# Window attention and a mixture of experts on one core: logits evicted ahead of values, values in block order, rows requested later

## The chip, the cores and the metric

The kernel runs on one core of one Trainium2 chip. A core has five engines that run their own instruction streams side by side: TensorE (PE; its weight loads are listed apart as PEld), VectorE (DVE), ScalarE (ACT), GpSimd (POOL) and SyncE (SP), which here issues most of the DMAs. Matmul results land in PSUM, everything else is in SBUF. The metric is the device time of one execution in microseconds (us).

## The reference

```python
# q, k, v: 8 batches x 8 heads x 576 positions x 64; N = 8*576 = 4608 tokens, D = 512, E = 8 experts, F = 1024
scores = (1 / np.sqrt(64)) * q @ k.transpose(0, 1, 3, 2)
rel = pos[:, None] - pos[None, :]
scores = np.where((rel >= 0) & (rel < 64), scores, -1e9)     # each position sees itself and the 63 before it
attn = softmax(scores)                                       # with 1e-9 added to the sum
x = (attn @ v).transpose(0, 2, 1, 3).reshape(N, D)

logits = x @ w_gate + modality_bias[modality_id]
e_idx = np.argmax(logits, axis=1)
gate_w = softmax(logits)[np.arange(N), e_idx]
for e in range(E):                                           # each token goes to one expert
    mask = e_idx == e
    out[mask] = gate_w[mask, None] * (np.maximum(x[mask] @ w1[e], 0) @ w2[e])
```

## The kernel before

**Attention.** The tokens are cut into 72 blocks of 64 positions; two neighbouring blocks make a pair of 128 tokens, and there are `NPR` = 36 pairs. The main loop (`for s in range(NPR + 4)`) is a software pipeline written out by hand: step s computes scores and their row minima for pair s (`scores`, `minima`), the exponentials (`exps`), the transposed probabilities of pair s-1 (`probs_t`, into `pT`), the products with the values of pair s-2 (`values`, eviction in `values_out`) and their transposes (`x_t`), and the gate's logits of pair s-3 (`logits`). Queries and keys of later pairs are transposed in between (`heads_t`, `heads_out`, into `qT` and `kT`). The program order on every engine is the order in which these functions are called; no scheduler reorders it.

`values` writes `av`, one PSUM bank of 128 tokens x 8 heads x 64. Its 32 matmuls (16 heads' halves for the upper, 16 for the lower 64 partitions; these two halves run side by side) write 64 neighbouring columns each, so that `av` is ordered by head. `values_out` takes the reciprocal of the 8 row sums `rs` and multiplies `av` by it into `xa`, in two VectorE instructions, one for each half a of a head's 64 columns. On the way it changes the order of the columns: `xa` holds, for g = head modulo 2 and a = first or second 32 columns of the head, 128 columns from the four heads of that g:

```python
to = xa[:, 0:DM].rearrange("p (g a c d) -> p a c g d", g=2, a=2, d=R32)
```

`x_t` then transposes the four blocks of 128 columns of `xa`, ScalarE copies them out as `xaT`, and a step later `logits` multiplies them by the gate's weights and adds the bias on VectorE into `lg` (line L694), out of PSUM. That PSUM tile is one of two that take turns under the name `tp` (`turn_bank`); in a step from 13 on the turns are: logits, probabilities for the first half of the heads, probabilities for the second half, the transposes of xa, then heads and routing. The second half's transposes so reuse the bank of the logits and have to wait for the eviction of those.

In a step, VectorE was given `values_out`, then the eviction of the logits, then the eight minima.

**Routing.** Every second step the logits of two pairs choose the experts (`route1` to `route3`), and the 256 rows `xa`, with gate and token number in two more columns, are scattered by an indirect DMA of GpSimd into `xs_scratch`, sorted by expert (L765).

**Experts.** A slot is 256 rows of one expert, computed in 16 pieces. Piece `first(k, i)` is 12 matmuls of the first layer (L304, into `em` or `sp`), piece `second(k, t)` 6 matmuls of the second (L326, into `y`). Weights and rows are split into a high and a low part (`Whi`, `Wlo`, `xh`, `xl`), and three products of parts are added up. The generator `slot_pieces` yields after each piece; from step `FIRST` = 12 on, each attention step has four gaps, and each `gap` runs one piece, so that a slot takes four steps. What follows a piece on the other engines goes through the list `later`. When the attention is over, the remaining slots run without gaps (there `last` is set).

The weights of two experts are loaded and split in the attention steps by `weights(s)`, in units of 128 x 512 (DMAs of L103 and L107 on SP, splits L114 on ScalarE and L119 on VectorE).

The rows of the next slot are requested by `fetch()` while the present slot is computed: SP reads the row number that VectorE worked out (L204) and issues five DMAs from `xs_scratch` into the tile `xt` (L211), of which there is one. Later `x_turn` transposes `xt` in 32 x 32 blocks on VectorE (L266), and `x_part` splits it into `xh` and `xl` (L195, L196) and has GpSimd copy gate and token number (L287, L289). Which slots may run during attention is fixed by `EARLY`: the table for a slot is worked out after the step that scattered its rows. The requests fall in steps 11, 14, 18, 22, 26, 30, 34 and 38; the slots of steps 14, 18 and 22 are planned in the step just before. A request on SP has to wait until the scatter of its rows has landed. In a slot of the attention steps, `fetch` stands before piece `first(2, 1)`, which is the second gap of its step, and `x_turn` follows piece `first(3, 1)`, in the second gap of the next step. Once `last` is set, `fetch` stands before `first(1, 0)`.

Of the kernel before, what the change touches and what calls it, by code (L numbers as in the profile page):

```python
# [8 lines left out]
F32 = mybir.dt.float32  # L9
# [4 lines left out]
ALU = mybir.AluOpType  # L14
# [5 lines left out]
P = 128  # L20
W64 = 64
# [5 lines left out]
def tile_window_attn_moe(  # L27
# [12 lines left out]
    nc = tc.nc  # L40
    B, H, S, D = q.shape
    N = B * S
    DM = H * D
    E = w_gate.shape[1]
    F = w1.shape[2]
    HP = H // 2
    R32 = 32
# [3 lines left out]
    NPR = NBLK // 2  # L51
# [15 lines left out]
    FIRST = 12  # L67
# [7 lines left out]
    NC1 = DM // P  # L75
# [153 lines left out]
    todo = []  # L229
    last = []  # L230
# [37 lines left out]
    def slot_pieces():  # L268
# [129 lines left out]
        NK = NC2 // 2  # L398
# [10 lines left out]
        while True:  # L409
            nxt = None  # L410
            for k in range(1, NK):
                for i in range(2):
                    if (k, i) == ((1, 0) if last else (2, 1)) or k == 2 and i == 1 and nxt is None:
                        assert todo
                        nxt = fetch()
                    first(sl, k, i)
                    if k == NK - 1 and i == (0 if last else 1):
                        later.append(lambda: x_turn(nxt))
                    yield
                for t in range(2):  # L420
                    second(sl, k - 1, t)
                    if k == NK - 1 and nxt and t == 1:
                        x_part(nxt, 1)
                    yield
                    if k == NK - 1 and nxt and t == 0:
                        x_part(nxt, 0)
                        run_later()
            second(sl, NK - 1, 0)
            yield
            if nxt["nb"] == 1:  # L430
                break
            first(nxt, 0, 0)
            yield
            first(nxt, 0, 1)
            yield
            second(sl, NK - 1, 1)
            yield
            sl = nxt
# [40 lines left out]
    small = actx.enter_context(tc.tile_pool(name="small", bufs=2))  # L479
# [18 lines left out]
    vo = {}  # L498
    ve = {}
    qk = {}  # L500
    st = {}
# [148 lines left out]
        nc.gpsimd.tensor_scalar(out=rs, in0=sm, scalar1=1e-9, scalar2=None, op0=ALU.add)  # L650


    def values(p):
        st.pop((p, "s"))
        av = st[p, "av"] = ps_a.tile([P, H, D], F32, name="av")
        for u in range(H):
            a, hp = divmod(u, HP)
            pT = st[p, "p", a]
            for c in range(2):
                i = hp * P + c * W64  # L660
                nc.tensor.matmul(  # L661
                    out=av[c * W64:(c + 1) * W64, 2 * hp + a], lhsT=pT[:, i:i + W64],
                    rhs=(vo if c else ve)[p][:, 2 * hp + a, :], start=True, stop=True)

    def values_out(p):
        rs = st.pop((p, "rs"))
        nc.vector.reciprocal(out=rs, in_=rs)
        xa = st[p, "xa"] = xas[p % XBUF]
        av = st.pop((p, "av")).rearrange("p (c g) (a d) -> p a c g d", g=2, a=2)
        to = xa[:, 0:DM].rearrange("p (g a c d) -> p a c g d", g=2, a=2, d=R32)  # L670
        for a in range(2):
            nc.vector.tensor_tensor(  # L672
                out=to[:, a], in0=av[:, a],
                in1=rs.rearrange("p (c g) -> p c g", g=2)[:, :, :, None].broadcast_to([P, NC1, 2, R32]), op=ALU.mult)

    def x_t(p, xp):
        xa = st[p, "xa"]
# [337 lines left out]
    for s in range(NPR + 4):  # L1015
        j = s % GB
        for f, args in at.pop(s, ()):
            f(*args)
        n_tick = 6 if s < FIRST else 5
        n_gap = 0 if s < FIRST else 4  # L1020
        G = s // GB + 1
        heads = PARTS[j] if G < NG else ()
        R = (s - 5) // GB if s >= 5 and j == 1 else -1
        if 1 <= s < FIRST:
            swap_upper(s - 1)

        if 2 <= s < NPR + 2:
            values(s - 2)
            values_out(s - 2)
        if 3 <= s < NPR + 3:  # L1030
            logits(s - 3, turn_bank(s) if s != FIRST else ps_m.tile([P, 512], F32, name="y0"))
            if (s - 3) % GB == GB - 1:
                route1((s - 3) // GB)
        if s < NPR:
            scores(s)
            if s == FIRST:
                x_turn(fetched[0])
                gap(it, True)
            minima(s)
            if s == FIRST - 2:  # L1040
                tick(todo[0][-1] - issued[0], table=True)
        if 1 <= s <= NPR:
            if s == FIRST:
                run_later()
            if s >= FIRST:
                swap_upper(s - 1)
            swap_v(s - 1)
            for a in range(2):
                probs_t(s - 1, a, turn_bank(s))
            sums(s - 1)  # L1050
        if s < NPR:
            exps(s, (0, 1))
        if s == 0:
            first_pair(1, (both[:1], both[1:]))
            cast_bias()
        if n_gap > 0 and s != FIRST:
            gap(it, True)
        if 2 <= s < NPR + 2:
            x_t(s - 2, turn_bank(s) if s != FIRST else ps_m.tile([P, 512], F32, name="y0"))
        run_later()  # L1060
        tick(2)
        if s < NPR:
            exps(s, (2, 3, 4))
        if n_gap > 0:
            if FIRST < s < FIRST + 4 or s % 2:
                weights(s)
            if s != FIRST:
                gap(it, True)
        if heads:
            tp = turn_bank(s)  # L1070
            heads_t(G, *heads[0], tp)
            heads_out(tp, G, *heads[0], nc.vector.tensor_copy)
        if s == FIRST:
            weights(s)
            gap(it, True)
        run_later()
        tick(n_tick)
        cnt = None
        if R >= 0:
            tp = turn_bank(s)  # L1080
            rk = route2(R, tp)
            if R == NG - 1 or any(R == T for T, _ in EARLY):
                cnt = counts_out(tab if R == NG - 1 else pl, counts(R, tp))
            route3(R, rk)
        if s < NPR:
            exps(s, (5, 6, 7))
        if n_gap > 2:
            if FIRST <= s < FIRST + 4:
                weights(s)
            gap(it, True)  # L1090
        if heads:
            tp = turn_bank(s)
            heads_t(G, *heads[1], tp)
            heads_out(tp, G, *heads[1], nc.scalar.copy if heads[1] == K1 else nc.vector.tensor_copy)
        run_later()
        tick(n_tick)
        if s == WEIGHTS:
            load_weights()
        if s >= WEIGHTS:
            weights(s)  # L1100
        if n_gap > 3:
            gap(it, True)
        run_later()
        if s == 1:
            select_bias()
        if s == 4:
            nc.sync.dma_start(out=xs_blk[DUMMY:DUMMY + 2].rearrange("b p c -> p b c"), in_=padrow)
        for T, xs_ in EARLY:
            if T == R:
                plan(T, xs_, cnt)  # L1110
# [270 lines left out]
```

## Time and profile before

| | |
|---|---|
| time, median of 3 runs | 629.67 us (629.13 to 629.82) |
| time of the profiled execution | 629.68 us |
| span of the profiled execution, first to last instruction | 627.8 us |
| mean granted TensorE clock | 0.994 |
| TensorE busy | 605.6 us (96%) |
| VectorE busy | 383.7 us (61%) |
| ScalarE busy | 298.5 us (48%) |
| GpSimd busy | 138.2 us (22%) |
| HBM traffic | 67.49 MB read, 23.91 MB written, 146 GB/s over the span |

Busy times of engines overlap, and a busy time is a sum over the whole program. The page also cuts the span into 40 equal slices and gives each engine's busy share of a slice in tenths. Attention alone takes about the first 81 us (steps 0 to 12), attention with experts' pieces goes on to about 352 us (steps 12 to 39), and the experts alone to the end. In a list of waits a line reads: engine, tile and line that waited, what released it, total us, how often, the longest. In a timeline a line reads: start, time taken, engine, line, operation, tiles (out<-in), shape, count, and in brackets the idle time before it and its releaser. Matmul ends are modelled.

### The profile page before, as it was taken

Reading aid. Unit: us, or ns where it says so; the run is one execution under the profiler, and the core shown is the slowest. Engines: PE = TensorE matmul, PEld = TensorE weight load, DVE = VectorE, ACT = ScalarE, POOL = GpSimd, SP = SyncE. Lnnn points to the kernel's source line nnn. Section 1 sums busy time; section 2 is a strip of 40 time slices with the busy share of each in tenths; the row PEclk is TensorE's granted clock in tenths of the full one; section 3 lists DMA queues with packets and bytes.
Section 4 is the critical chain, followed back from the end, with each engine's and each line's share of the span. In section 5 each row is a group of like instructions: output and inputs, shape, how many; then the busy total and the mean of one; then the engine's idle time right before and its main releaser. Section 6 shows DMA issues by size and latency. Waiting matters only on the chain.

```text
span 627.8 us, 17328 instructions
## 1 busy us (share of the span) xinstructions
PE 605.6 (96%) x6365; PEld 541.8 (86%) x6365; DVE 383.7 (61%) x1522; ACT 298.5 (48%) x933; POOL 138.2 (22%) x315
## 2 busy tenths in 40 slices
PE   8998879999999999999999999999999999999996
PEld 5887778889889888888988999999999999989986
DVE  4889988867766776757665275223324633876721
ACT  4899876665657556555644111111113522564411
POOL 6332322042222212320422220011011111102202
PEclk7999999999999999999999999999999999999999
DMA  9999864864674654553422133622062544677300
GB/s 164 207 229 238 203 186 139 212 170 120 169 202 124 177 125 112 143 135 87 128 61 84 53 102 101 226 78 69 13 190 78 164 162 124 194 247 234 125 13 24
DMA packets 158982, 88.07 MB, mean 140 GB/s; under 512 B 122618, under 2 KB 141616, under 8 KB 158768
## 3 DMA queue, kind: packets, MB, share of 16 engines
q1 hardware_dynamic: 150272, 67.45, 42.9%
q0 software_dynamic: 5888, 18.93, 8.0%
q8 instruction: 50, 0.82, 0.5%
q10 hardware_dynamic: 2736, 0.58, 0.5%
q14 instruction: 36, 0.29, 0.2%
HBM read 67.49 MB, written 23.91 MB: 146 GB/s over the span
## 4 chain that ended last, share of the span: by engine, by line
PE 50%; DVE 0%; issue 0%; POOL 0%; ACT 0%; POOLq 0%
PE y L326 23%; PE em L304 13%; PE sp L304 10%; PE tp L467 1%; PE y L377 1%; PE av L661 1%; PE sp L352 0%; PE em L352 0%; PE tp L689 0%; PE sp L609 0%; DVE xa L672 0%; POOL out_dram L390 0%; ACT pT L644 0%; POOLq L1258 0%; DVE y L388 0%
## 5 line engine op out<-in xcount | busy, mean ns | idle before, releaser
L326 PE MATMUL y<-Whi,hh 128*128 128x512 f32 x288 | 117.0, 406 | 0.0
L635 ACT ACTIVATE ss<-ss,mn 128x128 f32<-128x128 f32 x288 | 112.4, 396 | 5.2 <-DMA y<-in_moe_modality_id_dram 2.8
L326 PE MATMUL y<-Wlo,hh 128*128 128x512 f32 x288 | 112.8, 392 | 0.0
L326 PE MATMUL y<-Whi,hl 128*128 128x512 f32 x288 | 112.7, 391 | 0.0
L337 POOL DMA_INDIRECT out_dram<-y,id x36 | 39.8, 1104 | 238.0 <-DVE y L334 156.6
L313 DVE SCALAR_TENSOR_TENSOR hl<-em,hh 128x512 fp32r<-128x512 f32 x50 | 34.5, 690 | 92.9 <-ACT hh L312 91.4
L304 PE MATMUL em<-xh,Whi 128*128 128x256 f32 x400 | 83.8, 291 | 0.0
L312 ACT ACTIVATE hh<-em 128x512 fp32r<-128x512 f32 x50 | 29.5, 591 | 105.3 <-PE em L304 101.3
L304 PE MATMUL em<-xl,Whi 128*128 128x256 f32 x400 | 79.3, 280 | 0.0
L304 PE MATMUL em<-xh,Wlo 128*128 128x256 f32 x400 | 79.2, 280 | 0.0
L623 DVE CUSTOM_DVE_ANT_0 ss<-sp,masks 128x128 f32<-128x128 f32 x288 | 63.5, 286 | 7.2 <-PE sp L609 7.1
L644 ACT COPY pT<-tp 128x512 f32<-128x512 f32 x57 | 32.0, 588 | 75.3 <-PE tp L467 75.2
L326 PEld LDWEIGHTS y<-Whi,hl 128*128 128x128 f32 x288 | 54.1, 188 | 12.1
L304 PEld LDWEIGHTS em<-xh,Whi 128*128 128x128 f32 x400 | 62.4, 189 | 1.8
L326 PEld LDWEIGHTS y<-Whi,hh 128*128 128x128 f32 x288 | 54.2, 188 | 8.2
L326 PEld LDWEIGHTS y<-Wlo,hh 128*128 128x128 f32 x288 | 54.3, 188 | 7.8
L304 PEld LDWEIGHTS em<-xl,Whi 128*128 128x128 f32 x400 | 61.0, 188 | 0.0
L304 PEld LDWEIGHTS em<-xh,Wlo 128*128 128x128 f32 x400 | 60.9, 188 | 0.0
L635 ACT ACTIVATION_READ_ACCUMULATOR ss<-ss,mn 128x1 f32 x288 | 55.4, 192 | 0.0
L765 POOL DMA_INDIRECT xs_scratch<-xa,idx x36 | 36.3, 1009 | 84.9 <-DVE lm L708 27.2
L312 ACT ACTIVATE hh<-sp 128x512 fp32r<-128x512 f32 x22 | 13.2, 598 | 75.8 <-PE sp L304 75.8
L661 PEld LDWEIGHTS av<-ve,pT 128*64 128x64 f32 x576 | 36.3, 138 | 13.1 <-issue 7.5
(240 smaller groups left out, 1215.5 us busy)
## 6 DMA issues: line engine op xcount, KB each, us to landing
xt<-xs_scratch SPq DMA_DIRECT2D x72, 128.0 KB, 2.8
vo<-in_v_dram SPq DMA_DIRECT2D x32, 256.0 KB, 3.3
y<-in_moe_w_dram SPq DMA_DIRECT2D x32, 256.0 KB, 3.4
vo<-in_moe_w_dram SPq DMA_DIRECT2D x24, 256.0 KB, 4.6
ss<-in_moe_w_dram SPq DMA_DIRECT2D x24, 256.0 KB, 3.3
xs_scratch<-xs_scratch SPq DMA_DIRECT2D x8, 514.0 KB, 5.5
pT<-in_moe_w_dram SPq DMA_DIRECT2D x16, 256.0 KB, 4.2
qk<-in_k_dram SPq DMA_DIRECT2D x14, 256.0 KB, 4.0
```

The source lines that it names most:

```text
L304: nc.tensor.matmul(out=hb[:, i * TP:(i + 1) * TP], lhsT=w[buf][:, c0:c0 + P], rhs=x[:, c * TP:(c + 1) * TP], start=(n == 0), stop=(n == le ...
L312: nc.scalar.activation(out=hh, in_=hb, func=AF.Relu),
L313: nc.vector.scalar_tensor_tensor(out=hl, in0=hb, scalar=0.0, in1=hh.bitcast(F32), op0=ALU.max, op1=ALU.subtract)))
L326: nc.tensor.matmul(out=sl["y", t], lhsT=h[:, i * TP + t * P:i * TP + (t + 1) * P], rhs=w[buf][:, c0:c0 + DM], start=(k == 0 and n == 0), s ...
L337: ins = nc.gpsimd.indirect_dma_start(out=out, out_offset=bass.IndirectOffsetOnAxis(ap=sl["id"][:, t:t + 1], axis=0), in_=y, in_offset=None ...
L377: nc.tensor.matmul(out=yp[:, cols], lhsT=sl["h", n][lo][:, c * P:(c + 1) * P], rhs=w[buf][:, c0 + cols.start:c0 + cols.stop], start=(m == ...
L467: nc.tensor.transpose(out=out_, in_=in_, identity=ident[p0:p0 + n, p0:p0 + n])
L623: nc.vector.tensor_tensor_reduce(out=ss[a][:, hp, :], in0=sp[a][:, hp * P:(hp + 1) * P], in1=mask, scale=-1.0 / 8.0, scalar=3.0e38, op0=AL ...
L635: nc.scalar.activation(out=ss[a][:, hp, :], in_=ss[a][:, hp, :], func=AF.Exp, bias=mn[:, h:h + 1], scale=-1.0, accum_out=sm[:, h:h + 1])
L644: nc.scalar.copy(out=pT, in_=pp)
L661: nc.tensor.matmul(out=av[c * W64:(c + 1) * W64, 2 * hp + a], lhsT=pT[:, i:i + W64], rhs=(vo if c else ve)[p][:, 2 * hp + a, :], start=Tru ...
L765: ins = nc.gpsimd.indirect_dma_start(out=xs, out_offset=bass.IndirectOffsetOnAxis(ap=idx[:, j:j + 1], axis=0), in_=xg[j], in_offset=None)
```

## The change

Three edits, in one diff:

- `values` writes the products into `av` in the column order of `xa`, as two runs of 32 columns for each matmul. `values_out` then needs one multiplication of 128 x 512 in place of two of 128 x 256. The reciprocals are written four-fold ordered (16 instead of 8 for each token) so that they can be broadcast over runs of 32 columns.
- From step 13 on, `values_out` is called after `logits` (and `route1`, which only puts work on a list), not before. Up to step 12 the order stays.
- In the attention steps, `fetch` moves from before `first(2, 1)` to before `second(1, 1)`, from the second gap of its step to the fourth. `x_turn` stays where it was.

```diff
@@ slot_pieces
             for k in range(1, NK):
                 for i in range(2):
-                    if (k, i) == ((1, 0) if last else (2, 1)) or k == 2 and i == 1 and nxt is None:
-                        assert todo
+                    if k == 1 and i == 0 and last:
                         nxt = fetch()
+                        turn_at = 0
                     first(sl, k, i)
-                    if k == NK - 1 and i == (0 if last else 1):
+                    if k == NK - 1 and i == turn_at:
                         later.append(lambda: x_turn(nxt))
                     yield
                 for t in range(2):
+                    if k == 2 and t == 1 and nxt is None:
+                        nxt = fetch()
+                        turn_at = 1
                     second(sl, k - 1, t)
...
+    def by_block(x):
+
+        return x.rearrange("p h d -> p (h d)").rearrange("p (g a c d) -> p g a c d", g=2, a=2, d=R32)
+
     def values(p):
...
                 nc.tensor.matmul(
-                    out=av[c * W64:(c + 1) * W64, 2 * hp + a], lhsT=pT[:, i:i + W64],
-                    rhs=(vo if c else ve)[p][:, 2 * hp + a, :], start=True, stop=True)
+                    out=by_block(av)[c * W64:(c + 1) * W64, a, :, hp, :], lhsT=pT[:, i:i + W64],
+                    rhs=(vo if c else ve)[p][:, 2 * hp + a, :].rearrange("p (a d) -> p a d", a=2),
+                    start=True, stop=True)

     def values_out(p):
         rs = st.pop((p, "rs"))
-        nc.vector.reciprocal(out=rs, in_=rs)
+        rw = small.tile([P, 2, 2, HP], F32, name="rw")
+        nc.vector.reciprocal(
+            out=rw, in_=rs.rearrange("p (c g) -> p g c", g=2)[:, :, None, :].broadcast_to([P, 2, 2, HP]))
         xa = st[p, "xa"] = xas[p % XBUF]
-        av = st.pop((p, "av")).rearrange("p (c g) (a d) -> p a c g d", g=2, a=2)
-        to = xa[:, 0:DM].rearrange("p (g a c d) -> p a c g d", g=2, a=2, d=R32)
-        for a in range(2):
-            nc.vector.tensor_tensor(
-                out=to[:, a], in0=av[:, a],
-                in1=rs.rearrange("p (c g) -> p c g", g=2)[:, :, :, None].broadcast_to([P, NC1, 2, R32]), op=ALU.mult)
+        nc.vector.tensor_tensor(
+            out=xa[:, 0:DM].rearrange("p (x d) -> p x d", d=R32),
+            in0=st.pop((p, "av")).rearrange("p h d -> p (h d)").rearrange("p (x d) -> p x d", d=R32),
+            in1=rw.rearrange("p g a c -> p (g a c)")[:, :, None].broadcast_to([P, 2 * H, R32]), op=ALU.mult)
@@ main loop
         if 2 <= s < NPR + 2:
             values(s - 2)
-            values_out(s - 2)
+            if s <= FIRST:
+                values_out(s - 2)
         if 3 <= s < NPR + 3:
             logits(s - 3, turn_bank(s) if s != FIRST else ps_m.tile([P, 512], F32, name="y0"))
             if (s - 3) % GB == GB - 1:
                 route1((s - 3) // GB)
+        if FIRST < s < NPR + 2:
+            values_out(s - 2)
         if s < NPR:
             scores(s)
```

## Prediction

> **What bounds the kernel now.** I read the page first (busy time and the slices), then the windows by stage, then the waits of the stage in which TensorE idles, and last the timeline around those waits.
>
> ```profile
> PE 605.6 (96%) x6365; PEld 541.8 (86%) x6365; DVE 383.7 (61%) x1522; ACT 298.5 (48%) x933; POOL 138.2 (22%) x315
> PE   8998879999999999999999999999999999999996
> ```
> ```profile
> 20.00:81.00 61.00, 53.28 (x1025) 46.81 (x1024) 55.85 (x313) 54.55 (x212) 22.93 (x44) 1.00 0.95 224
> 81.00:352.00 271.00, 264.17 (x3392) 236.12 (x3392) 188.61 (x880) 158.08 (x548) 64.84 (x134) 1.00 0.51 136
> 352.00:609.00 257.00, 257.00 (x1671) 234.15 (x1668) 124.43 (x260) 73.59 (x134) 35.41 (x76) 1.00 0.43 131
> ```
>
> The window columns are stretch, length, and busy time of PE, PEld, DVE, ACT, POOL, then granted clock, DMA share and GB/s. There are three stages. From 352 us on (experts alone) PE is busy without a break at the full clock: this change has nothing to win there, and whatever earlier stages save arrives there unchanged. From 81 to 352 us (attention steps 13 to 37 with the experts' pieces between them) PE idles 271.00 - 264.17 = 6.8 us. Before 81 us (attention alone, steps 2 to 12) DVE is busy 55.85 of 61 us, more than PE.
>
> What PE and DVE wait for in the middle stage, and DVE's waits in the first (us in total, times, longest):
>
> ```profile
> DVE xa L672 <- PE av L661: 8.9, 11, 1.2
> DVE ss L623 <- PE sp L609: 5.4, 12, 0.5
> PE tp L467 <- DVE lg L694: 5.2, 8, 1.6
> PE tp L467 <- ACT pT L644: 3.4, 3, 2.0
> ```
> ```profile
> DVE xa L672 <- PE y L467: 1.5, 1, 1.5
> DVE ss L623 <- PE sp L609: 0.6, 1, 0.6
> DVE xa L672 <- PE av L661: 0.4, 1, 0.4
> ```
>
> So 5.2 of the 6.8 us in which PE stands still are eight transposes of probabilities that wait for the logits' eviction (L694), because they use the same PSUM bank. In the first stage DVE waits only 1.5 + 0.6 + 0.4 = 2.5 us, so nearly every DVE nanosecond saved there moves the whole program.
>
> **The change, part by part.**
>
> *1. Logits evicted first (steps 13 to 37).* The worst case is step 13: DVE comes late out of an expert's eviction, then does reciprocal, two halves of xa, and only then L694. The DVE rows, and the PE row that waits:
>
> ```profile
> 87.98 0.69 DVE L313 SCALAR_TENSOR_TENSOR hl<-em,hh 128x512 fp32r<-128x512 f32 x1 [0.82 <-ACT hh L312]
> 88.59 0.19 DVE L667 RECIPROCAL rs<-rs 128x8 f32<-128x8 f32 x1
> 88.87 0.88 DVE L672 TENSOR_TENSOR xa<-av,rs 128x256 f32<-128x256 f32 x2
> 89.67 0.15 DVE L694 TENSOR_TENSOR lg<-tp,bias_sel 128x8 f32<-128x8 f32 x1
> 89.74 0.28 DVE L623 CUSTOM_DVE_ANT_0 ss<-sp,masks 128x128 f32<-128x128 f32 x1
> ```
> ```profile
> 89.88 0.55 PE L467 MATMUL tp<-ident_r,ss 128*128 128x128 f32 x3 [1.55 <-DVE lg L694]
> 166.50 0.63 PE L467 MATMUL tp<-ident_r,ss 128*128 128x128 f32 x4 [1.09 <-DVE lg L694]
> 307.15 0.66 PE L467 MATMUL tp<-ident_r,ss 128*128 128x128 f32 x4 [0.20 <-DVE lg L694]
> ```
>
> L694 would take the reciprocal's place at 88.59 instead of 89.67: 1.08 us earlier. Of the eight waits only the first, 1.55, is longer than what is gained by that (0.47 stays); the second longest, 1.09, goes but for a hundredth; the last is the shortest. Upper bound: 5.2 - 0.5 = 4.7 us. Lower bound: 0, if PE merely meets another wait as early. What is late next: in these steps DVE is behind, and its own chain behind L694 (minima, then ScalarE's exponentials) hardly moves, so PE comes up to 1 us nearer to it. The waits list has no PE wait on kT, qT, hh or hl, and DVE is busy only 188.61 of 271 us, so I take most of it: 4.0 us.
>
> The price of the new order falls in the steps in which DVE is early and waits for values. Step 18:
>
> ```profile
> 141.57 0.19 DVE L667 RECIPROCAL rs<-rs 128x8 f32<-128x8 f32 x1
> 142.34 0.88 DVE L672 TENSOR_TENSOR xa<-av,rs 128x256 f32<-128x256 f32 x2 [0.57 <-PE av L661]
> 143.14 0.15 DVE L694 TENSOR_TENSOR lg<-tp,bias_sel 128x8 f32<-128x8 f32 x1
> 143.77 0.29 DVE L623 CUSTOM_DVE_ANT_0 ss<-sp,masks 128x128 f32<-128x128 f32 x1 [0.48 <-PE sp L609]
> ```
> ```profile
> 142.09 0.59 PE L689 MATMUL tp<-wg,xaT 128*64 128x8 f32 x16
> 142.61 1.10 PE L609 MATMUL sp<-kT,qT 64*64 64x128 f32 x32
> ```
>
> Now DVE idles until the logits end (142.09 + 0.59 = 142.68) with reciprocal, xa and minima queued behind. It runs L694 (89.74 - 89.67 = 0.07 until the next starts), the reciprocal (0.28 until xa may start, plus 0.05, below) and one eviction (0.60, below): 142.75 + 0.07 + 0.33 + 0.60 = 143.75, with some 0.07 taken for the signal from PE. The minima begin at 143.77 in any case, as they wait for the scores. Cost: nothing, with only hundredths of a microsecond of cover; without cover it would be some 0.5 us of DVE per such step, on an engine with 82 us free in this stage. I cost it at 0. The x transposes come a quarter step later. POOL and SP get no instruction from the moved function, so neither queue is reordered by this part.
>
> *2. One eviction for two, and a wider reciprocal (all 36 steps).*
>
> ```profile
> L672 DVE TENSOR_TENSOR xa<-av,rs x72: 424/425/426, 20.1 to 345.8; 128x256 f32<-128x256 f32 x72
> L667 DVE RECIPROCAL rs<-rs x36: 179/196/204, 19.8 to 344.9; 128x8 f32<-128x8 f32 x36
> ```
> ```profile
> L759 DVE RECIPROCAL xa<-se x36: 143/150/166, 39.2 to 363.8; 128x1 f32<-128x1 f32 x36
> ```
>
> Two evictions hold DVE from 88.87 to 89.67 = 0.80 us. A 512-wide one from PSUM holds it for 88.59 - 87.98 = 0.61 (the L313 row; I use 0.60). The reciprocal goes from 8 to 16 elements: (196 - 150)/7 = 6.6 ns an element, so +0.05. Net: 0.80 - 0.60 - 0.05 = 0.15 us a step. In steps 2 to 12 this is 11 x 0.15 = 1.6 us, of which I take 1.4, since DVE does wait at a few points there. From step 13 on it falls into DVE's free time: 0. The x transposes now wait for the whole eviction instead of its first half, but the whole ends 0.15 us before the second half did, and two of the four blocks needed that half anyway: 0.
>
> [...]
>
> *3. Strided products (L661).* Each product writes two runs of 32 columns instead of one of 64. No row shows TensorE writing runs. The nearest shows it reading them: half of the scores (L609, window of c = 0) read two blocks in descending order, half one piece, and all take the same:
>
> ```profile
> L609 PE MATMUL sp<-kT,qT x1152: 268/269/473, 8.4 to 326.7; 64*64 64x128 f32 x192
> ```
> ```profile
> 334.17 1.08 PE av L661 x32
> 343.60 1.08 PE av L661 x32
> ```
>
> Lower bound 0; a gain has no reason, as the columns stay. Upper bound: a run costs as much as a whole product of 64 columns, which doubles 1.08 us a step: over the 25 steps from 13 to 37, in which PE is the bound, 27 us. I take 0 by the scores' row, and keep part of the rest for the range.
>
> *4. Rows requested two pieces later.* This moves one register load and five DMAs on SP behind one or two weight loads, and the table's DVE instructions with them. The first slot of this kind:
>
> ```profile
> 108.23 2.48 SPq L211 DMA_DIRECT2D xt<-xs_scratch  x5
> 110.97 0.36 SPq L107 DMA_DIRECT2D y<-in_moe_w_dram  x1
> 111.63 1.02 SPq L103 DMA_DIRECT2D y<-in_moe_w_dram  x1
> ```
> ```profile
> SPq L211 <- DMA xs_scratch<-xa,idx: 11.2, 4, 4.2
> ```
> ```profile
> POOL gate L287 <- DMA xt<-xs_scratch: 35.7, 7, 7.2
> ```
> ```profile
> xt<-xs_scratch SPq DMA_DIRECT2D x72, 128.0 KB, 2.8
> ```
> ```profile
> 117.00 1.29 DVE L266 STREAM_TRANSPOSE xt<-xt 128x512 f32<-128x512 f32 x2
> ```
>
> The requests already sit up to 4.2 us on the scatter of the rows they read; two pieces (half of a step of 343.60 - 334.17 = 9.4 us, so some 5) mostly replace that wait, and let weight loads pass. Issued by 108.23 + 2.48 = 110.7 and landing 2.8 us later, the rows are there near 114 and needed at 117.00: 3 us of cover. The delay beyond today's is 5 - 4.2, so some 1 to 2 us: hidden, 0. GpSimd waits for the rows too (gate), and would wait that much longer; behind it on POOL is the next step's ve copy, which the products need only a step later. A gain has no place to appear, as neither PE nor DVE waits for a weight load in the lists above.
>
> **Sum.** 629.68 us is the profiled execution's time, 1.9 us more than its span of 627.8, and within 0.01 of the median 629.67. 629.7 - 4.0 - 1.4 = 624.3 us.
>
> **Rivals.**
>
> *A. The wait is only handed on.* PE, freed from L694, meets the next thing late: pT from ScalarE (already 3.4 us) or x transposes behind a later xa. For it: DVE gains 0.15 us a step where PE gains up to 1.08. Against: the other six waits average (5.2 - 1.55 - 1.09)/6 = 0.43 us, little to be late by, and DVE has free time. If two thirds are handed on: 629.7 - 1.4 - 1.3 = 627.0 us.
>
> *B. The runs cost PE time.* PE has next to no slack from 81 us on. 25 steps of 16 pairs (upper and lower half of the partitions) are 400 pairs, each 1.08/16 = 68 ns now. At 5.4/400 = 13.5 ns a pair the whole gain is gone; from there on it decides for slower, and at the full upper bound it gives 624.3 + 27 = 651 us. For it: nothing seen. Against: runs cost the scores nothing when read. [...]
>
> *C. Rows late.* If the two pieces came wholly on top, the rows would be 5 - 3 = 2 us late, and DVE, which runs in order, would hold the minima behind the x transposes. In the three slots that are planned just before their request that gives 624.3 + 6 = 630.3 us: slower. Against: the slip replaces a wait of similar size.
>
> **How the numbers follow.** Forecast 0.62 (own range 623.0 to 625.8); A 0.18; B without change 0.08, B slower 0.05; C 0.07. A change under 0.2% (1.26 us) cannot be told from none. Faster: 0.62 + 0.18 = 0.80; same: 0.08; slower: 0.12. The range runs from all of both bounds, 629.7 - 4.7 - 1.6 = 623.4, less 0.9 for DVE time that I counted at nothing, to B just short of cancelling, 629.5; that leaves out the 0.12.
>
> **What would show it.** L672: 36 of 128x512, about 690 ns; L667 about 250 ns. PE's wait on L694 falls from 5.2 to some 0.5 us, and the middle stage's PE idle time from 6.8 to about 3. The first expert piece of step 12 starts about 1.4 us earlier. The 32 products still take 1.08 us; if they take longer, B. A DVE wait of L266 on the rows' DMA would be C; new PE waits on pT or xa, A. The stage from the last attention step on stays as long as it is.

## The result and the profile after

| | before | after |
|---|---|---|
| time, median of 6 runs | 629.17 us (628.28 to 629.82) | 621.75 us (619.51 to 623.66) |
| ratio, 95% interval | | 0.9884 (0.986 to 0.9909) |
| time of the profiled execution | 629.68 us | 621.29 us |
| TensorE idle, 81 to 352 us | 6.8 us | 1.1 us |

The change makes the kernel 1.16% faster: 7.3 us by the ratio, 8.4 us by the two profiled executions. The prediction had the direction and the stages in which the time would be gained, but 5.4 us for the sum; 621.75 us lies just below its range, which ends at 623.4 - 0.9 = 622.5 us. The page and the windows of the changed kernel, columns as before:

```profile
span 619.6 us, 17314 instructions
PE 603.5 (97%) x6365; PEld 542.2 (88%) x6365; DVE 381.8 (62%) x1486; ACT 297.4 (48%) x933; POOL 139.7 (23%) x315
```
```profile
20.00:81.00 61.00, 54.10 (x1050) 48.35 (x1051) 57.16 (x307) 55.83 (x219) 24.38 (x46) 1.00 0.97 233
81.00:352.00 271.00, 269.88 (x3443) 243.01 (x3442) 187.77 (x859) 156.97 (x546) 67.82 (x138) 1.00 0.51 136
352.00:609.00 257.00, 257.00 (x1653) 233.14 (x1652) 124.92 (x254) 74.81 (x136) 34.00 (x72) 1.00 0.42 130
```

Only the middle row looks different: TensorE now stands still for 271.00 - 269.88 = 1.12 us. (The stage ends 8 us earlier now, so its last 8 us belong to the experts, where TensorE never idled.) TensorE's waits from 81 to 352 us (total, times, longest) say what became of the eight on the logits' eviction (L694, now L702; transposes L467 are now L470):

```profile
PE tp L470 <- ACT pT L647: 0.7, 1, 0.7
PE tp L470 <- DVE lg L702: 0.4, 1, 0.4
```

One of the eight is left, 0.4 us long. It is that of step 13, as VectorE's rows of that step and the transposes' row show:

```profile
86.62 0.69 DVE L313 SCALAR_TENSOR_TENSOR hl<-em,hh 128x512 fp32r<-128x512 f32 x1 [0.83 <-ACT hh L312]
87.23 0.16 DVE L702 TENSOR_TENSOR lg<-tp,bias_sel 128x8 f32<-128x8 f32 x1
87.31 0.24 DVE L676 RECIPROCAL rw<-rs 128x16 f32<-128x16 f32 x1
87.58 0.69 DVE L679 TENSOR_TENSOR xa<-av,rw 128x512 f32<-128x512 f32 x1
88.19 0.28 DVE L626 CUSTOM_DVE_ANT_0 ss<-sp,masks 128x128 f32<-128x128 f32 x1
```
```profile
87.44 0.66 PE L470 MATMUL tp<-ident_r,ss 128*128 128x128 f32 x4 [0.41 <-DVE lg L702]
```

The logits' eviction now stands right behind L313, at 0.61 us after its start (87.23 - 86.62), where before it stood at 1.69 us (89.67 - 87.98); the difference is the 1.08 us that the prediction worked out. The two groups of `values_out` (durations min/median/max):

```profile
L676 DVE RECIPROCAL rw<-rs x36: 230/244/255, 20.4 to 336.9; 128x16 f32<-128x16 f32 x36
L679 DVE TENSOR_TENSOR xa<-av,rw x36: 691/691/692, 20.8 to 337.5; 128x512 f32<-128x512 f32 x36
```

**Where the time came from.** A step is measured here from the start of its first product with the values (L661, now L668) to that of the next step, in single records of the two traces. Up to the start of step 13 the changed kernel has gained 1.30 us, from step 13 to step 37 it gains 7.01 us, and from there to the last matmul nothing (279.1 us before, 279.2 after). The 1.30 us can't be told from chance: over the traces of all kernels of this document step 13 starts anywhere from 82.7 to 87.3 us, and on average no earlier with the single eviction than with two. From step 14 on a step without a stop has the same length in all of these traces, within 0.03 us, so that there single traces can be compared. Every step from 13 to 36 that is not in this table has the same length in both, within 0.02 us:

| step | 13 | 17 | 20 | 21 | 24 | 25 | 28 | 29 | 33 | 36 | sum |
|---|---|---|---|---|---|---|---|---|---|---|---|
| idle recorded before, us | 1.55 | 0.24 | 1.09 | 0.34 | 0.77 | 0.78 | 0 | 0.21 | 0.19 | 0.68 | 5.85 |
| idle recorded after, us | 0.41 | 0 | 0 | 0 | 0 | 0 | 0 | 0 | 0 | 0 | 0.41 |
| step shorter by, us | 1.14 | 0.45 | 1.27 | 0.55 | 0.96 | 0.99 | 0.18 | 0.39 | 0.41 | 0.67 | 7.01 |

Two things in this table are not in the prediction. First, in the seven steps in which a stop on the logits vanishes as a whole (17, 20, 21, 24, 25, 29 and 33) the step gains about 0.2 us more than the idle time that it loses, and step 28 gains 0.18 us with no idle time recorded at all. Second, step 36 has lost a stop that was not on the logits.

The 0.2 us can be read from the rows. Two groups of four transposes of the probabilities, with the stop of step 24 between them before, and in one row without it after:

```profile
208.82 0.66 PE L467 MATMUL tp<-ident_r,ss 128*128 128x128 f32 x4
210.25 0.63 PE L467 MATMUL tp<-ident_r,ss 128*128 128x128 f32 x4 [0.77 <-DVE lg L694]
```
```profile
204.12 1.09 PE L470 MATMUL tp<-ident_r,ss 128*128 128x128 f32 x8
```

Before, the eight take 210.25 + 0.63 - 208.82 = 2.06 us, after 1.09 us: 0.97 us, against 0.77 us idle. One transposition is recorded as 0.273 us long, but in the stream the next one starts 0.109 us later. Idle time is counted from the recorded end, so the first 0.164 us of this stop hide under it; and the first matmul behind a stop has its successor 0.136 us later instead of 0.109. 0.164 + 0.027 = 0.19 us. Recorded ends are modelled, but the starts of the products, from which the table's last row comes, are not. A short stop can leave no idle time at all. In step 28 before, the eight transposes stand in one row, but take 0.19 us more than in step 24 after:

```profile
253.02 1.28 PE L467 MATMUL tp<-ident_r,ss 128*128 128x128 f32 x8
```

### The profile page after: what moved, and what is told of

Its sections match the earlier page's. It is cut to its first block, busy times and chain, and to the rows that moved or that the text cites. A ratio compares the mean times of both kernels' runs of the same rounds, so it can differ in the third digit from the quotient of the medians.

```text
span 619.6 us, 17314 instructions
## 1 busy us (share of the span) xinstructions
PE 603.5 (97%) x6365; PEld 542.2 (88%) x6365; DVE 381.8 (62%) x1486; ACT 297.4 (48%) x933; POOL 139.7 (23%) x315
## 5 line engine op out<-in xcount | busy, mean ns | idle before, releaser
L313 DVE SCALAR_TENSOR_TENSOR hl<-em,hh 128x512 fp32r<-128x512 f32 x50 | 34.5, 690 | 92.8 <-ACT hh L312 82.1
L304 PE MATMUL em<-xl,Whi 128*128 128x256 f32 x400 | 79.3, 280 | 0.0
L312 ACT ACTIVATE hh<-sp 128x512 fp32r<-128x512 f32 x22 | 13.2, 598 | 75.9 <-PE sp L304 73.9
L668 PEld LDWEIGHTS av<-ve,pT 128*64 128x64 f32 x576 | 36.3, 138 | 13.2 <-issue 8.2
```

The lines of the kernel that those rows point to most:

```text
L304: nc.tensor.matmul(out=hb[:, i * TP:(i + 1) * TP], lhsT=w[buf][:, c0:c0 + P], rhs=x[:, c * TP:(c + 1) * TP], start=(n == 0), stop=(n == le ...
L312: nc.scalar.activation(out=hh, in_=hb, func=AF.Relu),
L313: nc.vector.scalar_tensor_tensor(out=hl, in0=hb, scalar=0.0, in1=hh.bitcast(F32), op0=ALU.max, op1=ALU.subtract)))
L668: nc.tensor.matmul(out=by_block(av)[c * W64:(c + 1) * W64, a, :, hp, :], lhsT=pT[:, i:i + W64], rhs=(vo if c else ve)[p][:, 2 * hp + a, :] ...
```

## The experiments

The questions were: which part of the change gives which part of the gain; is the extra of 0.2 us a fixed price of each stop; do the 32-column runs cost TensorE anything; how much of VectorE's time in the first stage moves the program; and what made step 36 shorter. Lines are those of each kernel. "Trace" is one profiled execution, read against that of before or after; where a gain is given in us for timed runs, the interval behind it is 95%.

### The order alone

```diff
         if 2 <= s < NPR + 2:
             values(s - 2)
-            values_out(s - 2)
+            if s <= FIRST:
+                values_out(s - 2)
...
+        if FIRST < s < NPR + 2:
+            values_out(s - 2)
```

> Only the order is changed (logits evicted ahead of values from step 13); products, two evictions and requests as before. Theory 1 (a stop of TensorE costs the recorded idle time and about 0.2 us more, for the stream has to start again): the eight recorded waits lose some 4.8 us of idle time and 8 x 0.2 = 1.6 us more, and step 36, where the framework now gives the second half's probabilities another bank, another 0.7 us: 7.0 us faster than before, about 622.2 us; products of step 13 begin when they did before. Theory 0 (the recorded idle time is the cost, as the prediction had it): 4.8 + 0.7 = 5.5 us faster, about 623.7 us. Rival A (the wait is handed on): 1.5 to 3 us faster. In the step table a removed wait of I us must move the next step by I + 0.2 under theory 1 and by I under theory 0.

Measured 623.59 us (6 runs), ratio 0.9911 (0.9891 to 0.9931): 5.6 us faster (4.3 to 6.9). That is less than the 7.0 us of theory 1, and by itself it would speak for theory 0, with 5.5 us. The steps decide. In the trace every step from 14 to 36 has the changed kernel's length: they lost 4.30 us of recorded idle time and are 5.86 us shorter than before, against 5.87 in the changed kernel. Step 13 can't be read here: in step 12 of this execution TensorE's clock fell to half (0.52 granted from 82 to 85 us, last section), and steps 12 and 13 together took 24.15 us, 1.07 us more than before. Whether the timed runs lost time in the same way is not on record. TensorE's waits from 81 to 352 us:

```profile
PE tp L467 <- ACT pT L644: 0.7, 1, 0.7
```

So the gain from step 14 on is the order's, all of it, and nothing took the place of the eight waits. (The wait of 0.7 us is that of step 16, which the kernels before and after have too.)

### The layout and the single eviction alone

The diff is the hunk of `by_block`, `values` and `values_out`, with the main loop and `slot_pieces` as before.

> Only the layout is changed: products in block order, one eviction of 128x512, reciprocal of 16; order and requests as before. Theory 1: the first stage (VectorE busy nearly throughout) gets 0.15 us a step for eleven steps, 1.6 to 1.9 us, and nothing after step 13, except that the eight waits on the logits' eviction, which still stands behind values, shrink by 0.15 us each where they are longer, up to 1.2 us: 1.6 to 3 us faster, 626.2 to 627.6 us. If writing two runs costs TensorE anything (rival B), the 32 products take more than 1.08 us and the time from step 13 on grows by 25 times that. If the first stage is not bound by VectorE: no change.

Measured 626.62 us (10 runs), ratio 0.9953 (0.9936 to 0.997): 3.0 us faster (1.9 to 4.0). From step 14 to 37 its trace is 1.53 us shorter: the stops on the logits stay, each shorter by what `values_out` saves. Step 24 is the example (0.77 before; its releaser is now named as pT, whose copy ends last by then):

```profile
207.69 0.63 PE L467 MATMUL tp<-ident_r,ss 128*128 128x128 f32 x4 [0.63 <-ACT pT L644]
```

This 1.5 us is no addition to the order's gain, which removes the same stops altogether. What is added is the rest, 3.0 - 1.5 = 1.5 us, uncertain by 1.1, up to step 13. That it arises in the first stage is inferred, not seen: between steps 3 and 12 the traces with the single eviction take 49.2 to 51.3 us (leaving out the one with more work added below) and those with two evictions 49.5 to 52.4. Order and layout together should then give 5.6 + 1.5 = 7.1 us; the changed kernel gives 7.3, and both sums are uncertain by more than the difference.

### The later request alone, and the change without it

```diff
-                    if (k, i) == ((1, 0) if last else (2, 1)) or k == 2 and i == 1 and nxt is None:
+                    if k == 1 and i == 0 and last:
...
+                    if k == 2 and t == 1 and nxt is None:
```

> Only the requests of rows are moved by two pieces; the rest as before. Theory 1 and the prediction: no change beyond 0.3 us, for no engine waits for what SP is held up in. If the later request frees the weight loads in a way that counts, faster by 0.5 us or more; if the rows come late (rival C), slower by up to 6 us, with VectorE waiting for the rows before it transposes them.

Measured 629.67 us (12 runs), ratio 1.0002 (0.9989 to 1.0015): no effect that the runs can tell, from 0.7 us faster to 0.9 us slower. Its trace has steps 14 to 36 longer than before by 0.87 us in all, from the stops in steps 16, 21 and 33; the first two are on the copy pT there. One execution doesn't show whether the request does this, and in the changed kernel steps 21 and 33 have no stop.

> The changed kernel without the later request of rows. Theory 1: the same time as the changed kernel, 621.5 to 622 us, 7.4 us faster than before, for the request is worth nothing. If the request gives part of the gain, this one lies 0.5 us or more above the changed kernel's 621.75.

Without the later request the change takes 621.33 us (4 runs), ratio 0.9868 (0.9844 to 0.9891), which cannot be told from the whole change. SyncE's queue shows what the request did do. Over the whole program its waits on the scatter of the rows were 13.2 us in 5 before, 11.2 of them from 81 us on; in the changed kernel:

```profile
SPq L211 <- DMA xs_scratch<-xa,idx: 1.6, 1, 1.6
```

The queue stands still less on the scatter, and the times show nothing gained by it.

### The runs of 32 columns alone

```diff
-                    out=av[c * W64:(c + 1) * W64, 2 * hp + a], lhsT=pT[:, i:i + W64],
-                    rhs=(vo if c else ve)[p][:, 2 * hp + a, :], start=True, stop=True)
+                    out=by_block(av)[c * W64:(c + 1) * W64, a, :, hp, :], lhsT=pT[:, i:i + W64],
+                    rhs=(vo if c else ve)[p][:, 2 * hp + a, :].rearrange("p (a d) -> p a d", a=2),
+                    start=True, stop=True)
```

`values_out` keeps its two evictions, which read `av` in the new order.

> The kernel before, with only the products' layout changed: they write two runs of 32 columns in block order, and the two evictions of 128x256 and the reciprocal of 8 stay (the evictions now read one half of each block). Theory 1: 32 products take 1.08 us as before, no change in time beyond 0.3 us. Rival B: 32 products take longer, by 0.06 us for each ns that a run costs, and the time grows by 25 times that.

Measured 629.86 us (10 runs), ratio 1.0002 (0.9992 to 1.0013). The chain of waits has the 32 products at the old duration:

```profile
322.38 1.08 PE av L665 x32
332.12 1.08 PE av L665 x32
```

Writing two runs of 32 columns costs TensorE nothing that shows; rival B is excluded. Only the output's layout was varied.

### The logits' eviction made late again, in eight steps

The changed kernel, with two sums that nobody uses on VectorE ahead of the logits' eviction:

```diff
+        if p + 3 in (17, 21, 24, 25, 28, 29, 32, 33):
+            for _ in range(2):
+                nc.vector.reduce_sum(out=slow, in_=masks.rearrange("p m i -> p (m i)"), axis=AX.X)
         nc.vector.tensor_tensor(
             out=st[G, "lg"][:, j, :], in0=lt[:, 0:E], in1=bias_sel[:, p, :], op=ALU.add)
```

> The changed kernel, with two sums over 384 columns put ahead of the logits' eviction on VectorE in steps 17, 21, 24, 25, 28, 29, 32 and 33 (their result is not used). Each sum should take 0.4 to 0.5 us, so that the eviction comes some 0.9 us later and TensorE stops again in steps 24 and 25 (some 0.6 us recorded as idle there, less in 17 and 21). Theory 1: against the changed kernel, step to step, TensorE loses the recorded idle time plus about 0.2 us in each such step, and in steps whose stop is under 0.2 us it loses time with no idle time recorded. Theory 0: it loses the recorded idle time and no more.

Stops came back in six of the eight steps (in 28 and 32 VectorE was early enough). In five of them the transposes start right behind the logits' eviction; in step 21 that eviction has ended 0.58 us before them, and it is the copy pT that ends just before them, as where both halves share a bank (see "Banks strictly in turn"). Each added sum, and the stop of step 25:

```profile
L704 DVE TENSOR_REDUCE slow<-masks x16: 530/550/554, 132.9 to 305.8; 128x1 f32<-128x384 f32 x16
```
```profile
221.37 0.66 PE L470 MATMUL tp<-ident_r,ss 128*128 128x128 f32 x4 [0.69 <-DVE lg L705]
```

| step | 17 | 21 | 24 | 25 | 29 | 33 |
|---|---|---|---|---|---|---|
| idle recorded, us | 0.19 | 0.73 | 0.73 | 0.69 | 0.11 | 0.10 |
| step longer than in the changed kernel, us | 0.41 | 0.93 | 0.91 | 0.93 | 0.30 | 0.29 |
| difference | 0.22 | 0.20 | 0.18 | 0.24 | 0.19 | 0.19 |

The difference is 0.18 to 0.24 us whether 0.10 or 0.73 us were recorded: a fixed price of each stop, not a share of its length. It also shows the cause in the other direction: the eviction of the logits made late brings the stops back. (The sums delay what follows on VectorE as well, but the five stops end with the logits' eviction. The one run took 628.97 us, 7.7 us more than the changed kernel's profiled execution: 3.8 us are from these steps, 2.8 came before step 14, with half the clock for 3.4 us in step 12 (0.86 granted from 76 to 88 us, last section), 0.4 in step 16 and 0.7 behind step 37.)

### One more VectorE instruction in each step of the first stage

```diff
     def values_out(p):
+        if p + 2 <= FIRST:
+            nc.vector.reduce_sum(out=slow, in_=masks.rearrange("p m i -> p (m i)"), axis=AX.X)
```

> The changed kernel, with one sum over 384 columns (not used) more on VectorE in each of steps 2 to 12, ahead of values' reciprocal: eleven times 0.4 to 0.5 us more work in the first stage. If VectorE sets the pace there, as the prediction had it: 4 to 5 us slower than the changed kernel, some 626 us. If the first stage is paced by something else (the loads of q, k, v and weights, ScalarE): 0 to 2 us.

Measured 625.76 us (6 runs), ratio 0.9947 (0.9932 to 0.9961). The sum's group and an instance with its successor:

```profile
L675 DVE TENSOR_REDUCE slow<-masks x11: 547/553/554, 20.4 to 78.1; 128x1 f32<-128x384 f32 x11
```
```profile
52.87 0.55 DVE L675 TENSOR_REDUCE slow<-masks 128x1 f32<-128x384 f32 x1
53.34 0.24 DVE L678 RECIPROCAL rw<-rs 128x16 f32<-128x16 f32 x1
```

It holds VectorE for 53.34 - 52.87 = 0.47 us, 5.2 us in 11 steps. By the ratios the program became (0.9947 - 0.9884) x 629.5 = 4.0 us longer, with some 1.8 us of uncertainty. So about three quarters of VectorE's time there moves the end, and by the uncertainty anything from two fifths to all of it; that fits the 1.4 of 1.6 us that the prediction took, within this wide margin. A single trace cannot show it: from step 3 to 12 the traces differ by 1 us and more between kernels that are the same there (51.29 us before, 49.51 with the order alone, which changes nothing ahead of step 13).

### The split of the rows behind the probabilities in step 12

TensorE's longest stop in the changed kernel, 1.85 us, is in step 12, where it waits for ScalarE's copy pT, which stands behind the split of the first rows (`run_later`). Here the split is put behind the transposes of the probabilities:

```diff
-            if s == FIRST:
-                run_later()
             if s >= FIRST:
                 swap_upper(s - 1)
...
                 probs_t(s - 1, a, turn_bank(s))
+            if s == FIRST:
+                run_later()
```

> The changed kernel, with the split of the first slot's rows (xh, xl) put behind the transposed probabilities in step 12, no longer ahead of them. In step 12 TensorE stops for 1.9 to 3.3 us for pT, which ScalarE writes only after xh, which waits for the rows. If that stop is what costs, it shortens to well under 1 us, and the step from 12 to 13 takes 0.4 to 1.5 us less than the 10.4 us of the changed kernel; the granted clock, which was halved after a stop of 3 us in two executions, stays at 1.00 there. 0.5 to 1.5 us faster than the changed kernel, some 620.5 us. If TensorE merely stops at the first expert piece instead, for xh and xl: no change.

Measured 622.58 us (6 runs), ratio 0.9885 (0.9868 to 0.9902): no gain over the changed kernel. TensorE still stands still for 1.82 us, from 79.28 to 81.10 us, now ahead of the expert's piece that needs the split. That stop is handed on, as rival A had it for the logits. The clock, which was expected to stay whole there, fell to half behind this stop too (0.86 granted from 76 to 88 us, last section).

### Banks strictly in turn

Why did step 36 lose a stop on pT? The two banks do not take turns in every step as the description of the kernel before has it: the framework chooses the bank of each `tp` tile, and by what rule is not on record. The waits tell what it chose. In step 36 before, the second half of the probabilities waited for the copy of the first, so both had the same bank; with the order alone changed, it no longer waits for that copy, so it has the logits' bank. In step 16 the halves share a bank in both kernels. Three kernels set the banks by a written list:

```diff
-    ps_t = actx.enter_context(tc.tile_pool(name="ps_t", bufs=2, space=PSUM))
+    ps_tt = [actx.enter_context(tc.tile_pool(name=f"ps_t{i}", bufs=1, space=PSUM)) for i in range(2)]
...
-        return ps_t.tile([P, 512], F32, name="tp")
+        b = int(TURNS[n_turn[0]])
+        n_turn[0] += 1
+        return ps_tt[b].tile([P, 512], F32, name="tp")
```

The kernel before, with the halves of steps 16 and 36 on two banks:

> The kernel before with one thing changed: its two transposing PSUM banks are taken strictly in turn by a written list, where before the halves of the probabilities share a bank in step 16 and in step 36 (the second half then waits for ScalarE's copy pT of the first). Theory (step 36's part of the gain is that bank and nothing of the logits' order): the pT waits of 0.68 us in steps 16 and 36 are gone, steps 16 and 36 are 0.67 us shorter each, all others as before: 1.3 us less, ratio 0.998. Rival (the stop in step 36 comes from the late logits or from ScalarE being late, whatever the bank): both steps keep their length, ratio 1.000.

The changed kernel, with the halves of step 16 on two banks:

> The changed kernel with the banks strictly in turn, which differs from it only in step 16 and in the names of the banks from there on. Theory: the pT wait of 0.68 us in step 16 is gone and the stage from step 13 to 37 is 0.67 us shorter, 621.1 us in the middle of runs that spread over some 4 us, so it is read from the trace. Rival: the wait moves to the eviction of the logits, which now share their bank with the other half: a wait of L702's kind appears in step 16 and the stage is as long.

The changed kernel, with the halves of step 36 on one bank again:

> The changed kernel with the second half of the probabilities in step 36 put on the bank of the first again, as the kernel before had it. Theory: the stop of 0.68 us returns, step 36 is 0.67 us longer than in the changed kernel and nothing else in the stage from step 13 to 37 changes: 622.4 us. Rival (step 36 gained by the earlier logits): step 36 stays at 8.76 us.

Measured 632.07 us (12 runs, ratio 1.003, 1.0009 to 1.0052), 623.16 us (5 runs, 0.988, 0.9844 to 0.9916) and 623.44 us (6 runs, 0.9883, 0.9853 to 0.9913). The expectation of the first failed, theory and rival both: the kernel became slower. In the second its rival came out, as the wait moved to the logits' eviction (L708); in the third its theory did, as the stop of 0.68 us came back. The first one's stops in steps 16 and 36:

```profile
124.17 0.63 PE L469 MATMUL tp<-ident_r,ss 128*128 128x128 f32 x4 [1.78 <-DVE lg L700]
339.00 0.63 PE L469 MATMUL tp<-ident_r,ss 128*128 128x128 f32 x4 [1.11 <-DVE lg L700]
```

Step 16 with banks in turn in the changed kernel, and step 36 with the shared bank in it:

```profile
119.35 0.63 PE L472 MATMUL tp<-ident_r,ss 128*128 128x128 f32 x4 [1.01 <-DVE lg L708]
```
```profile
331.72 0.66 PE L472 MATMUL tp<-ident_r,ss 128*128 128x128 f32 x4 [0.68 <-ACT pT L653]
```

| idle recorded in the step, us (length of the step) | halves share a bank | second half on the logits' bank |
|---|---|---|
| step 36, logits behind the values | 0.68 (9.43) | 1.11 (9.86) |
| step 36, logits ahead of the values | 0.68 (9.43) | 0 (8.76) |
| step 16, logits behind the values | 0.68 (11.36) | 1.78 (12.43) |
| step 16, logits ahead of the values | 0.68 (11.36) | 1.01 (11.66) |

Step 36 needed both: its gain of 0.67 us comes from the logits' bank, but that bank is worth having only once the logits leave it early. In step 16 the shared bank is the better one before. In the changed kernel that is not shown: there step 16 varies between executions with the shared bank (11.36 us in the table, but 11.49, 11.72 and 12.11 in the traces of the shared bank in step 36, the late eviction and the split behind the probabilities). Why step 36 gained only 0.67 and not 0.68 + 0.2: even in the changed kernel the eight transposes of step 36 take longer than the 1.09 us of step 24, a small stop under the recorded ends:

```profile
327.96 1.31 PE L470 MATMUL tp<-ident_r,ss 128*128 128x128 f32 x8
```

No version tried is faster than the changed kernel by more than the runs can tell.

## Why the prediction was wrong in size and right in kind

**Logits evicted first: 4.0 us taken, 7.0 us found in the trace. This term failed, and its upper bound of 4.7 us with it.** (The timed runs of the order alone, 5.6 us with 4.3 to 6.9, exclude the 4.0; that the bound of 4.7 fell is read from the steps.) Which wait goes, where, and what stays was right: 5.2 us of recorded waits became 0.4 in step 13, against 0.5 foreseen, and TensorE's idle time from 81 to 352 us fell to 1.1 us, against some 3. The step that failed is to set the price of a stop equal to its recorded idle time. Without step 36 the steps gained 7.01 - 0.67 = 6.34 us for 1.14 + 3.62 = 4.76 us of recorded idle (step 13, where a stop remains, and the seven others that had some); the other 1.58 us are the fixed price of seven stops at about 0.2 us and step 28's 0.18. The second error is the discount from 4.7 to 4.0, for waits handed on to pT or the transposes of xa: none was handed on. The third is that the wait on pT in step 36 (one of the 3 in 3.4 us that the prediction quotes) was taken as untouched, as the prediction did not ask who shares the bank: 0.67 us.

**One eviction for two, and a wider reciprocal: 1.4 us taken, about 1.5 us found, give or take 1.1** (3.0 us alone, less 1.5 us of the order's stops). So close an agreement is luck. So is that of a sign named for it: the first expert piece of step 12 starts 1.37 us earlier in this pair of traces (80.34 against 81.71 us), but anywhere from 79.3 to 82.5 us in the other traces with two evictions. L679 took 691 ns against 690 foreseen, L676 244 ns against 250: (244 - 196)/8 = 6.0 ns an element, near the 6.6 that the prediction worked out from rows. Nothing from step 13 on was right only because the order had already removed the stops.

**Strided products: 0 taken, 0 found**, by a run of their own. **Rows two pieces later: 0 taken, none found that the runs can tell**, by two runs. The cover was thinner than foreseen, though. The first such request and the transposes that need its rows, after:

```profile
107.96 3.45 SPq L211 DMA_DIRECT2D xt<-xs_scratch  x5
```
```profile
114.56 1.29 DVE L266 STREAM_TRANSPOSE xt<-xt 128x512 f32<-128x512 f32 x2
```

The last DMA is issued by 111.41 us, and with the median of 2.8 us that the kernel before shows until its rows land, they are there at 114.2, an estimate, as this trace does not tell when they landed; the transposes came at 114.56, not 117.00. By that estimate 0.3 us of the 3 us is left. VectorE did not wait for them.

**The rivals.** A (the wait is only handed on) is false: the order alone has no new wait from step 14 on. B is false by the runs of 32 columns alone. C is false. The sign named for it, a wait of L266 on the rows, does appear once:

```profile
393.70 1.31 DVE L266 STREAM_TRANSPOSE xt<-xt 128x512 f32<-128x512 f32 x2 [0.90 <-DMA xt<-xs_scratch]
```

But that is in the stage of the experts alone, where the request was not moved and TensorE did not stop, and the change without the later request has the same wait, of 0.86 us at 395.6 us.

**The sum.** In the two traces: 7.0 + 1.3 = 8.3 of the 8.4 us, of which the 1.3 is within chance. The timed runs give 7.3 us (5.7 to 8.8), and 5.4 lies below that. With 7.0 in place of 4.0 the prediction's own sum gives 621.3 us. The own range of the forecast, 623.0 to 625.8, was drawn around the discounted waits, and the wide range's lower end around the same undervalued bound.

## What to carry to other kernels

Price a stop of a pipelined engine by the distance between the starts of the work on both sides of it, less the same distance where it runs through; the recorded idle time leaves out the overlap of one instruction with the next, here about 0.2 us a stop. Put a small instruction that frees a buffer for the bottleneck engine ahead of the long ones on its in-order queue, and look at every wait on the buffers that take turns with it, not only at the wait that names it. Two buffers strictly in turn are not always the better choice: here strict turns made step 16 of the kernel before 12.43 - 11.36 = 1.07 us longer, and what counted was which of the two came free first at that point.

## What the runs showed of the hardware that was not expected

TensorE's clock stood at half in step 12, during or behind its longest stop, in some executions and not in others. The order alone, stop and windows from 79 us on (the last three columns are granted clock, DMA share, GB/s):

```profile
80.11 0.66 PE L467 MATMUL tp<-ident_r,Whi 128*128 128x128 f32 x4 [3.28 <-ACT pT L644]
```
```profile
79.00:82.00 3.00, 1.89 (x14) 1.89 (x15) 2.90 (x17) 3.00 (x11) 0.00 (x0) 0.91 1.14 267
82.00:85.00 3.00, 3.00 (x17) 3.00 (x16) 2.77 (x8) 3.00 (x15) 0.78 (x2) 0.52 0.42 118
```

Seven of the thirteen traces show this, with stops of 1.82 to 3.32 us, and by their records of the clock it lasts 3.4 us each time, from 81.5 to 84.9 us here; the mean granted clock from 76 to 88 us is 0.86 in all seven. (In an eighth, that with one more VectorE instruction a step, it lasts 6.8 us, from 75.3 us on, and the mean is 0.75.) At half the clock 3.4 us cost at most half of that, 1.7 us, an estimate. Before and after, with stops of 2.00 and 1.85 us there, kept the clock at 1.00, and so did the changed kernel with banks in turn, behind 2.44 us; the kernel before with banks in turn lost it (0.50 from 82 to 85 us) behind a stop of 2.00 us. So the same stop of 2.00 us came with half the clock in one execution and not in another, and what decides it is not shown here.

The opening shows the same. In six of the traces, before and after among them, the clock stood at half for 3.4 or 6.8 us between 8 and 20 us (the mean granted clock from 3 to 20 us is 0.90 or 0.80), and step 2 started at 17.7 to 20.0 us; in the other seven, at 1.00, it started at 16.5 to 17.2 us. After, and the order alone, which kept its clock there:

```profile
8.00:16.00 8.00, 7.26 (x90) 6.37 (x88) 5.99 (x37) 4.37 (x20) 3.03 (x14) 0.57 1.09 182
```
```profile
8.00:16.00 8.00, 6.32 (x100) 5.09 (x101) 6.94 (x48) 5.06 (x21) 3.23 (x15) 1.00 0.99 176
```

Part of the spread between the runs of one kernel (619.5 to 623.7 us after) may be this; it wasn't tried by itself and stays open.
